# Wider stationary values, a split of the lower parts, and a moved division in an attention and two-network kernel

## The chip, the cores and the metric

The kernel runs on one core of a Trainium2 chip. The metric is the device time of one execution in microseconds (us), the median of several runs.

## The reference

Three stages follow each other. The first is an attention with feature maps: for every head, `proj = x @ w_phi` is shifted by its largest absolute value per token, and the features are `exp` of it and of its negative, side by side. Keys and values are summed up into one matrix per head, and queries read from that.

```
q_p, k_p = phi(q), phi(k)                    # 8 batches, 8 heads, 576 tokens, 2 x 128 features
kv  = einsum('bhsf,bhsd->bhfd', k_p, v)
num = einsum('bhsf,bhfd->bhsd', q_p, kv)
den = einsum('bhsf,bhf->bhs', q_p, k_p.sum(2)) + 1e-6
x   = num / den                              # 4608 tokens of 512
```

The second stage sends each token to one of eight expert networks (or past them), the third is `(h - tanh(h)) @ w_out` with `h = x @ w_in`. All is float32.

## The kernel before, in words

The attention runs as 32 steps over `i`. A step treats two heads of one batch. Two batches share nine tiles of 128 tokens, so a step with even `i` takes five tiles, the last of which counts for 64 tokens only, and a step with odd `i` takes 64 tokens of that same tile, kept in slot 4, and then four full tiles (`slots_of`, L295). The loop is software pipelined: step `i` finishes batch and heads `i`, and prepares `n = i + 1`. The order in which each engine works is the order in which the calls stand in the loop; waits between engines come from the data.

Products are taken in pieces: a float32 is split into a rounded upper part (type FP32R) and the rest, the lower part, and a product is upper x upper, upper x lower and lower x upper. So there are `kh`/`kl`, `qh`/`ql` (`split_qk`, L226), `vh`/`vl` (`split_v`, L239, on GpSimd), and `kph`/`kpl` for the features of the keys: `exp_k` (L269) and `high_kp` (L273) run on ScalarE, `low_kp` (L277) on VectorE, each once for either sign `s`.

TensorE's order in step `i` is: `project(n, "k")` (L245), which fills the PSUM tile `proj`; `transpose_q(i, 0)` (L283); `key_value(i)` (L300); `transpose_q(i, 1)`; the first two tiles of `project(n, "q")`, which overwrite `proj`; `key_value_t(i)` (L315), which multiplies the turned `kv` by a small matrix; the rest of `project(n, "q")`; in one step of eight the two counts of `route_count` (L438); `numerator(i)` (L326) into the PSUM tile `num`. `key_value` forms, per head, three products over the five slots, 15 matmuls in one accumulation: 65 columns of `vh` or `vl` (64 values and a one) are stationary, 256 features move, and 64 or 128 rows (tokens) are summed over.

VectorE's order is: `shift(n, "k")` (L256: maximum over `proj` and subtraction into `dk`), `divide(i - 1)` (L338: reads `num`, writes rows of `x` and of the gate logits), a part of `narrow` (L190, which turns the weights of the last stage from doubles into float32), a part of the routing (L368 to L459), the copy of `kv` from PSUM (L323), `shift(n, "q")`, and `low_kp` for both signs. GpSimd does `kl`, `vh` and `vl`, `ql`, two operations of `narrow` (L212, L213) and the scatters of finished rows. `proj`, `num`, `kvb`, `kph` and `kpl` exist once.

Behind the loop come the expert networks and the last network, which the diff touches in comments only.

Of the kernel before, what the change touches and what calls it, by code (L numbers as in the profile page):

```python
# [8 lines left out]
F32 = mybir.dt.float32  # L9
F32R = mybir.dt.float32r  # L10
# [3 lines left out]
ALU = mybir.AluOpType  # L14
# [5 lines left out]
P = 128  # L20
# [8 lines left out]
NCH = SP // P  # L29
# [8 lines left out]
NSEG = 6144  # L38
BIG = 65536.0

# columns of the constants
C_ID = 0
C_TRI = 128
C_ONE = 256
# [15 lines left out]
def attention_moe_moe_kernel(  # L60
# [52 lines left out]
        eng.dma_start(raw[j // 2][:, o : o + 2048], src(s))  # L113

    def load_w(src, j, when):
        # half of the weights
        with tc.If(when > 0):
            for a in (2 * j, 2 * j + 1):
                load_part(src, a)
# [7 lines left out]
    def expert_w(i):  # L127
        return lambda s: wall[bass.ds(i, 1), :, s].rearrange("o p f -> (o p) f")

# [1 line left out]
    actx = ExitStack()  # L131
    rctx = ctx.enter_context(ExitStack())
    rt = rctx.enter_context(tc.tile_pool(name="route", bufs=1, side="right"))
# [13 lines left out]
    wpl = ap.tile([P, 2 * NF], F32R, name="wpl")  # L147
    wpr = ap.tile([P, 2 * NF], F32, name="wpr")
    wg = ap.tile([P, H, VE], F32, name="wg")
    vh = ap.tile([P, NCH, 2, VD], F32R, name="vh")  # L150
    vl = ap.tile([P, NCH, 2, VD], F32R, name="vl")
    kph = ap.tile([P, NCH * 2, 2, NF], F32R, name="kph")
    kpl = ap.tile([P, NCH * 2, 2, NF], F32R, name="kpl")
    ke = ap.tile([P, NCH * 2, 2, NF], F32, name="ke")
# [13 lines left out]
    st = {}  # L168
    NS = 4 * B

    # Two batches share nine tiles of 128 tokens: an even step takes the first five, an odd step
    # the other four and the fifth's second half, which stays in slot 4.
    def tiles(i):
        return NCH - i % 2

# [12 lines left out]
            )  # L188

    def narrow(w, e, m, x, dve=False):  # L190
        # a double's two words -> the nearest float32, |w| below 2**-106 to 0
        w = w.rearrange("p (n t) -> p n t", t=2)
        low, high = w[:, :, 0].bitcast(U32), w[:, :, 1].bitcast(U32)
        nc.vector.tensor_scalar(  # L194
            out=e, in0=high, scalar1=0x7FF00000, scalar2=None, op0=ALU.bitwise_and
        )
        nc.vector.tensor_scalar(  # L197
            out=m, in0=high, scalar1=0xFFFFF, scalar2=None, op0=ALU.bitwise_and
        )
        yield  # L200
        nc.scalar.activation(e, e, AF.Relu, scale=8.0, bias=bias[:, 0:1])
        nc.scalar.activation(x, low, AF.Identity, scale=2.0**-32, bias=bias[:, 1:2])  # L202
        if not dve:
            nc.scalar.copy(m.bitcast(F32), m)
        yield
        nc.vector.scalar_tensor_tensor(  # L206
            out=e, in0=high, scalar=0x80000000, in1=e, op0=ALU.bitwise_and, op1=ALU.bitwise_or
        )
        if dve:
            nc.vector.tensor_tensor(out=x, in0=x, in1=m, op=ALU.add)  # L210
        else:
            nc.gpsimd.tensor_tensor(out=x, in0=x, in1=m.bitcast(F32), op=ALU.add)  # L212
        nc.gpsimd.tensor_tensor(out=x, in0=x, in1=e.bitcast(F32), op=ALU.mult)  # L213
        yield
# [23 lines left out]

    def split_v(i):  # L239
        n = tiles(i)  # L240
        src = st[i]["v"][:, :n].rearrange("p c (h w) -> p c h w", h=2)
        nc.gpsimd.tensor_copy(vh[:, :n], src)
        nc.gpsimd.tensor_tensor(out=vl[:, :n], in0=src, in1=vh[:, :n].bitcast(F32), op=ALU.subtract)

    def project(i, w, lo_c=0, hi_c=NCH):  # L245
        hi, lo = st[i][w + "s"]
# [22 lines left out]
    def exp_k(i, s):  # L269
        n = tiles(i) * 2  # L270
        nc.scalar.activation(ke[:, :n, s], st[i]["dk"][:, :n], AF.Exp, scale=1.0 - 2.0 * s)

    def high_kp(i, s):  # L273
        n = tiles(i) * 2
        nc.scalar.copy(kph[:, :n, s], ke[:, :n, s])

    def low_kp(i, s):  # L277
        n = tiles(i) * 2
        nc.vector.tensor_tensor(  # L279
            out=kpl[:, :n, s], in0=ke[:, :n, s], in1=kph[:, :n, s].bitcast(F32), op=ALU.subtract  # L280
        )

# [10 lines left out]
            nc.scalar.activation(qp[h][:, s, :n], t[:, :n], AF.Exp, scale=1.0 - 2.0 * s)  # L293

    def slots_of(i):  # L295
        # slots in the order of the tokens, and the partitions that belong to the batch
        full = [(c, slice(0, P)) for c in range(4)]
        return [(4, slice(64, P))] + full if i % 2 else full + [(4, slice(0, 64))]

    def key_value(i):  # L300
        for h in range(2):
            n = 0
            for a, b in ((vh, kph), (vl, kph), (vh, kpl)):
                for c, q in slots_of(i):
                    nc.tensor.matmul(
                        kvb[:VD, h * 256 : h * 256 + 256], a[q, c, h],
                        b[q, 2 * c + h].rearrange("p s f -> p (s f)"),
                        start=n == 0, stop=n == 3 * NCH - 1,
                    )
                    n += 1  # L310
# [2 lines left out]
        nc.scalar.copy(kvt[i % 2][:VD], kvb[:VD])  # L313

    def key_value_t(i):  # L315
        # [feature, value | 1 | value . gate and skip weights]
        for a in range(4):
            nc.tensor.matmul(
                kvb[:, a * VE : a * VE + VE], kvt[i % 2][:, a * NF : a * NF + NF],
                wg[:, i % 8 // 2 * 2 + a // 2], start=True, stop=True,  # L320
            )
        kv = sm.tile([P, 4 * VE], F32, name="kv")
        nc.vector.tensor_copy(kv, kvb[:, : 4 * VE])  # L323
        st[i]["kv"] = kv
# [162 lines left out]
        return cnt, key  # L487

    def first_expert():
        # head: expert, rows of it already placed (256 at most), first row, second tile's row  # L490
        v = nc.vector
        cnt, key = counts_key()
        mx = rt.tile([P, 1], F32, name="kmx")
        v.tensor_reduce(out=mx, in_=key, axis=AX.X, op=ALU.max)
        v.tensor_tensor(out=forced, in0=key, in1=mx.to_broadcast([P, E]), op=ALU.is_equal)
        t = rt.tile([P, E], F32, name="kt")
        v.tensor_tensor(out=t, in0=forced, in1=cst[:, C_EID : C_EID + E], op=ALU.mult)
        v.tensor_reduce(out=head[:, 0:1], in_=t, axis=AX.X, op=ALU.add)
        v.tensor_reduce(out=head[:, 1:2], in_=cnt, axis=AX.X, op=ALU.max)
        v.tensor_scalar(  # L500
            out=head[:, 1:2], in0=head[:, 1:2], scalar1=float(NEARLY), scalar2=None, op0=ALU.min
        )
        v.tensor_scalar(
            out=head[:, 2:3], in0=head[:, 0:1], scalar1=float(CAP), scalar2=None, op0=ALU.mult
        )
        v.tensor_scalar(
            out=head[:, 3:4], in0=head[:, 1:2], scalar1=-float(P), scalar2=0.0, op0=ALU.add, op1=ALU.max
        )
        v.tensor_copy(headi, head)

    def block_table():
        # for each tile of 128 rows: its first row in xs, in x2s, whether an expert starts, the
        # next expert, whether there is one, whether there is none, all tiles
        v = nc.vector
        cnt, key = counts_key()
        done = rt.tile([P, E], F32, name="done")
# [96 lines left out]
        nc.vector.tensor_copy(mt, kvb[:7, :MAXT])  # L613

    def gather_index(seg0):
        # slot -> row of x2s: the first expert's early rows lie in front
        v = nc.vector
        low = rt.tile([P, 3], F32, name="low")
        t = rt.tile([P, E], F32, name="lowt")
# [42 lines left out]
    nc.vector.memset(num[64:, :, (NCH - 1) * VE : NCH * VE], 1.0)  # L662
    for t in kvt:
        nc.gpsimd.memset(t[64:], 0.0)
    split_qk(0, "k", nc.vector)
    split(wpr, wph, wpl)
    project(0, "k")
# [25 lines left out]
    for i in range(NS):  # L693
        n = i + 1
        more = n < NS
        if more:
            project(n, "k")
        if more:
            shift(n, "k")
        if i:  # L700
            divide(i - 1)
        if i == NS - 2:
            ldctx.close()
            bx = rctx.enter_context(tc.tile_pool(name="rows", bufs=1, side="right"))
# [38 lines left out]
        key_value(i)  # L743
        keep_key_value(i)
        if more:
            exp_k(n, 0)
        transpose_q(i, 1)
        if more:
            split_v(n)
            load(n + 1, "v")  # L750
            project(n, "q", 0, QC)
            exp_k(n, 1)
        key_value_t(i)
        if more:
            project(n, "q", QC)
        exp_q(i, 1)
        if more:
            high_kp(n, 0)
            shift(n, "q")
            low_kp(n, 0)  # L760
            high_kp(n, 1)
            low_kp(n, 1)
        else:
            t = pp.tile([P, NCH, 2 * NF], F32, name="proj")
            for c, a in ((0, xr), (1, xt)):
                for k in range(4):
                    nc.tensor.transpose(
                        t[:, 2 * c + k // 2, k % 2 * P : k % 2 * P + P], a[:, k * P : k * P + P], ident
                    )
            split(  # L770
                t[:, :4].rearrange("p (c a) (b f) -> p c (a b f)", c=2, b=2),
                xTh.rearrange("p c k f -> p c (k f)"), xTl.rearrange("p c k f -> p c (k f)"),
            )
# [27 lines left out]
    divide(NS - 1)  # L801
    actx.close()

# [1 line left out]
    wp2 = ctx.enter_context(tc.tile_pool(name="weights2", bufs=1))  # L805
    wh.append(wp2.tile([P, 4096], F32R, name="wh1"))
    wl.append(wp2.tile([P, 4096], F32R, name="wl1"))
    with ExitStack() as bctx:
# [51 lines left out]
            nc.sync.dma_start(x2s[bass.ds(r, P), :], yo)  # L860

        def split_up(half, k, eng):
            # columns of the next expert's first matrix that no later product reads
            cols = slice(half * 512, half * 512 + 512)
            w = [a.rearrange("p (k f) -> p k f", k=4)[:, k : k + 2, cols] for a in (raw[0], wh[0], wl[0])]
            split(*w, eng)
# [81 lines left out]
            nc.vector.tensor_copy(xt, xu)  # L948
    rctx.close()

# [1 line left out]
    op = ctx.enter_context(tc.tile_pool(name="ffw", bufs=1))  # L952
    o2 = ctx.enter_context(tc.tile_pool(name="ff2", bufs=2))
    ph = ctx.enter_context(tc.tile_pool(name="fph", bufs=2, space=PSUM))
# [112 lines left out]
def _layout(np, inputs):  # L1067
    f = np.float32
    q, k, v = (np.asarray(inputs[n]) for n in ("q", "k", "v"))

    # step pairs (two batches, two heads): 1152 tokens
    def feature_major(a):
        t = a.reshape(NPAIR, 2, H // 2, 2, S, DH).transpose(0, 2, 3, 5, 1, 4)
        return t.reshape(NPAIR * H // 2, P, 2 * S)
# [69 lines left out]
```

## Time and profile before

| | |
|---|---|
| three runs | 1605.92, 1611.25, 1613.95 us (median 1611.25) |
| profiled execution | span 1604.1 us (the page has no other time of it) |
| busy: TensorE, weight loads | 1549.3 us (97%), 1286.0 us (80%) |
| busy: VectorE, ScalarE, GpSimd | 839.5 (52%), 630.0 (39%), 393.8 us (25%) |
| granted TensorE clock, mean | 0.987 |

In the profile PE stands for matmuls on TensorE, PEld for loads of the stationary operand, which overlap them; DVE is VectorE, ACT ScalarE, POOL GpSimd. An entry such as `128*65 128x256` is a matmul with 128 rows and 65 stationary columns and an operand of 128 x 256 that moves. A time in front of a timeline row is the start in us from the beginning of the span, the next number is the duration in us. Ends of matmuls are modelled, so their durations overlap; the distance of two starts is the better measure. "L305" is line 305 of the kernel.

### The profile page before, as it was taken

How to read it: one execution, taken by the hardware profiler on the slowest of the kernel's cores; microseconds unless marked ns; L12 is line 12 of the kernel's file. 1: busy time of each engine (PE TensorE's matmuls, PEld its weight loads, DVE VectorE, ACT ScalarE, POOL GpSimd, SP SyncE). 2: the span in 40 equal slices, each digit the busy share in tenths (PEclk: the TensorE clock that was granted, in tenths of full speed). 3: DMA queues.
4: the chain of work that ended last, by engine and by line, in shares of the span. 5: the costliest groups of instructions: out<-in, count | busy, mean ns of one | idle time of the engine just before them, and what ended most of it. 6: DMA issues, size and time to landing. Idle time of an engine off the chain costs nothing.

```text
span 1604.1 us, 23498 instructions
## 1 busy us (share of the span) xinstructions
PE 1549.3 (97%) x8421; PEld 1286.0 (80%) x8421; DVE 839.5 (52%) x1179; ACT 630.0 (39%) x944; POOL 393.8 (25%) x288
## 2 busy tenths in 40 slices
PE   7999999999999999999599999999999999999999
PEld 6888888888887787877488888888888888888887
DVE  5788988988986525435587423232322323232322
ACT  5656556566564123415365322222222222222222
POOL 4444474474466202203423200000000000000000
PEclk9999999999999999999799999999999999999999
DMA  4344365244246513233433201010100101000000
GB/s 148 120 151 158 131 229 200 66 153 159 65 143 231 204 46 137 68 115 137 161 110 117 79 1 53 0 53 0 53 1 7 46 0 54 0 27 1 27 1 27
DMA packets 53576, 139.56 MB, mean 87 GB/s; under 512 B 5488, under 2 KB 5616, under 8 KB 50416
## 3 DMA queue, kind: packets, MB, share of 16 engines
q1 hardware_dynamic: 47152, 116.31, 21.3%
q0 software_dynamic: 5760, 18.90, 3.7%
q10 hardware_dynamic: 576, 3.15, 0.5%
q8 instruction: 59, 0.97, 0.2%
q14 instruction: 29, 0.24, 0.0%
HBM read 86.15 MB, written 52.19 MB: 86 GB/s over the span
## 4 chain that ended last, share of the span: by engine, by line
PE 45%; DVE 2%; POOL 1%; issue 1%; ACT 1%; DMA 0%; POOLq 0%
PE h L1013 22%; PE acc L1029 22%; POOL raw L213 1%; PE xtr L1002 1%; DVE wol L97 1%; DVE raw L210 1%; ACT woh L96 0%; DMA raw<-x2s,gidx 0%; DVE raw L206 0%; POOL raw L971 0%; DVE raw L194 0%; DVE wl L97 0%; ACT raw L202 0%; DVE raw L197 0%; DVE g L1017 0%
## 5 line engine op out<-in xcount | busy, mean ns | idle before, releaser
L1017 DVE TENSOR_TENSOR g<-h,g 128x512 f32<-128x512 f32 x144 | 99.5, 691 | 389.3 <-ACT g L1016 389.3
L1016 ACT ACTIVATE g<-h 128x512 f32<-128x512 f32 x144 | 85.8, 596 | 391.1 <-PE h L1013 391.1
L1013 PE MATMUL h<-x2Th,wh 128*128 128x512 f32 (+1 forms) x580 | 225.8, 389 | 0.0
L1013 PE MATMUL h<-x2Tl,wh 128*128 128x512 f32 (+1 forms) x580 | 225.6, 389 | 0.0
L1013 PE MATMUL h<-x2Th,wl 128*128 128x512 f32 (+1 forms) x580 | 225.6, 389 | 0.0
L1029 PE MATMUL acc<-woh,gh 128*128 128x512 f32 x576 | 225.5, 392 | 0.0
L1029 PE MATMUL acc<-woh,gl 128*128 128x512 f32 x576 | 224.2, 389 | 0.0
L1029 PE MATMUL acc<-wol,gh 128*128 128x512 f32 x576 | 224.1, 389 | 0.0
L333 PE MATMUL num<-kv,qp 128*128 128x74 f32 (+1 forms) x1280 | 151.9, 271 | 3.1 <-DVE kv L323 3.0
L97 DVE TENSOR_TENSOR gl<-g,gh 128x512 fp32r<-128x512 f32 x144 | 101.1, 702 | 98.9 <-ACT gh L96 98.9
L333 PEld LDWEIGHTS num<-kv,qp 128*128 128x128 f32 (+1 forms) x1280 | 139.7, 180 | 14.6 <-DVE kv L323 4.9
L971 POOL DMA_INDIRECT raw<-x2s,gidx x36 | 35.4, 982 | 428.1 <-PE xtr L1002 416.0
L96 ACT CAST gh<-g 128x512 fp32r<-128x512 f32 x144 | 89.4, 621 | 111.0 <-DVE g L1017 111.0
L1013 PEld LDWEIGHTS h<-x2Th,wh 128*128 128x128 f32 x580 | 109.9, 189 | 22.3
L1013 PEld LDWEIGHTS h<-x2Tl,wh 128*128 128x128 f32 x580 | 109.8, 189 | 22.3
L1013 PEld LDWEIGHTS h<-x2Th,wl 128*128 128x128 f32 x580 | 109.7, 189 | 22.3
L1029 PEld LDWEIGHTS acc<-woh,gl 128*128 128x128 f32 x576 | 108.1, 188 | 22.5
L1029 PEld LDWEIGHTS acc<-wol,gh 128*128 128x128 f32 x576 | 108.2, 188 | 22.0
L1029 PEld LDWEIGHTS acc<-woh,gh 128*128 128x128 f32 x576 | 108.1, 188 | 21.9
L279 DVE TENSOR_TENSOR kpl<-ke,kph 128x1280 fp32r<-128x1280 f32 (+1 forms) x64 | 119.9, 1916 | 0.0
L97 POOL TENSOR_TENSOR wl<-raw,wh 128x1024 fp32r<-128x1024 f32 x25 | 66.5, 2682 | 211.8 <-PE y L845 200.8
L293 ACT ACTIVATE qp<-tq 128x640 f32<-128x640 f32 (+1 forms) x128 | 75.6, 643 | 90.6 <-PE tq L287 90.6
(203 smaller groups left out, 2775.6 us busy)
## 6 DMA issues: line engine op xcount, KB each, us to landing
raw<-in_wall_dram SPq DMA_DIRECT2D x20, 1024.0 KB, 5.8
raw<-in_w_dram SPq DMA_DIRECT2D x30, 512.0 KB, 3.7
x2s<-raw SPq DMA_DIRECT2D x12, 1024.0 KB, 5.9
x2s<-x SPq DMA_DIRECT2D x4, 2304.0 KB, 9.6
out_dram<-raw SPq DMA_DIRECT2D x36, 256.0 KB, 3.8
v<-in_vx_dram SPq DMA_DIRECT2D x16, 325.0 KB, 3.0
k<-in_kT_dram SPq DMA_DIRECT2D x16, 320.0 KB, 4.3
q<-in_qT_dram SPq DMA_DIRECT2D x16, 320.0 KB, 3.8
```

The costliest lines, as they stand in the source:

```text
L96: nc.scalar.copy(hi, src)
L97: eng.tensor_tensor(out=lo, in0=src, in1=hi.bitcast(F32), op=ALU.subtract)
L210: nc.vector.tensor_tensor(out=x, in0=x, in1=m, op=ALU.add)
L213: nc.gpsimd.tensor_tensor(out=x, in0=x, in1=e.bitcast(F32), op=ALU.mult)
L279: nc.vector.tensor_tensor(out=kpl[:, :n, s], in0=ke[:, :n, s], in1=kph[:, :n, s].bitcast(F32), op=ALU.subtract)
L293: nc.scalar.activation(qp[h][:, s, :n], t[:, :n], AF.Exp, scale=1.0 - 2.0 * s)
L333: nc.tensor.matmul(o, qp[h][:, s, slot, q], kv[:, a * VE : a * VE + VE], start=s == 0, stop=s == 1,)
L971: nc.gpsimd.indirect_dma_start(out=xg[:, t, :], out_offset=None, in_=x2s[:, :], in_offset=bass.IndirectOffsetOnAxis(ap=gidx[:, b * TB + t ...
L1013: nc.tensor.matmul(p[:, s], a[:, o : o + P], b[:, k, s], start=n == 0, stop=n == 11)
L1016: nc.scalar.activation(g, p, AF.Tanh)
L1017: nc.vector.tensor_tensor(out=g, in0=p, in1=g, op=ALU.subtract)
L1029: nc.tensor.matmul(acc[t], a[:, s], b[:, m], start=m == 0 and n == 0, stop=m == NM - 1 and n == 2)
```

## The change

`vh` and `vl` become flat, with 63 columns of zeros behind them (P - VD), and `key_value` loads 128 columns from the place where the 65 of its slot and head begin. The product then fills all 128 rows of `kvb`; only the first 65 are read, as before. `low_kp` takes an engine; the one for `s = 1` goes to GpSimd, and the order of the calls for the features of the keys changes with it. `divide(i - 1)` stands ahead of `shift(n, "k")`.

```diff
-    vh = ap.tile([P, NCH, 2, VD], F32R, name="vh")
-    vl = ap.tile([P, NCH, 2, VD], F32R, name="vl")
+    vh = ap.tile([P, NCH * 2 * VD + P - VD], F32R, name="vh")
+    vl = ap.tile([P, NCH * 2 * VD + P - VD], F32R, name="vl")
...
     def split_v(i):
         n = tiles(i)
-        src = st[i]["v"][:, :n].rearrange("p c (h w) -> p c h w", h=2)
-        nc.gpsimd.tensor_copy(vh[:, :n], src)
-        nc.gpsimd.tensor_tensor(out=vl[:, :n], in0=src, in1=vh[:, :n].bitcast(F32), op=ALU.subtract)
+        src = st[i]["v"][:, :n].rearrange("p c w -> p (c w)")
+        hi, lo = vh[:, : n * 2 * VD], vl[:, : n * 2 * VD]
+        nc.gpsimd.tensor_copy(hi, src)
+        nc.gpsimd.tensor_tensor(out=lo, in0=src, in1=hi.bitcast(F32), op=ALU.subtract)
...
-    def low_kp(i, s):
+    def low_kp(i, s, eng=nc.vector):
         n = tiles(i) * 2
-        nc.vector.tensor_tensor(
+        eng.tensor_tensor(
...
                 for c, q in slots_of(i):
+                    o = (2 * c + h) * VD
                     nc.tensor.matmul(
-                        kvb[:VD, h * 256 : h * 256 + 256], a[q, c, h],
+                        kvb[:, h * 256 : h * 256 + 256], a[q, o : o + P],
...
+    for t in (vh, vl):
+        nc.gpsimd.memset(t.bitcast(F32)[:, NCH * 2 * VD :], 0.0)
...
             project(n, "k")
+        if i:
+            divide(i - 1)
         if more:
             shift(n, "k")
-        if i:
-            divide(i - 1)
...
         keep_key_value(i)
         if more:
-            exp_k(n, 0)
+            exp_k(n, 1)
         transpose_q(i, 1)
         if more:
             split_v(n)
             load(n + 1, "v")
             project(n, "q", 0, QC)
-            exp_k(n, 1)
+            high_kp(n, 1)
+            low_kp(n, 1, nc.gpsimd)
         key_value_t(i)
         if more:
             project(n, "q", QC)
         exp_q(i, 1)
         if more:
+            exp_k(n, 0)
+            shift(n, "q")
             high_kp(n, 0)
-            shift(n, "q")
             low_kp(n, 0)
-            high_kp(n, 1)
-            low_kp(n, 1)
```

## Rows read from the trace of the kernel before

**Rows 1.** The page: the span and the number of instructions.
```profile
span 1604.1 us, 23498 instructions
```

**Rows 2.** Busy time by stretch: stretch, length, engines (instructions), clock, DMA share, GB/s.
```profile
276.00:340.00 64.00, 62.93 (x478) 53.44 (x477) 59.82 (x80) 38.38 (x54) 33.37 (x25) 1.00 0.31 102
```

**Rows 3.** Waits from 0 to 530 us: who for whom, total, times, longest.
```profile
PEld kvb L305 <- issue: 36.3, 193, 0.3
...
PE num L333 <- DVE kv L323: 3.0, 5, 1.7
...
PE kvb L441 <- DVE kv L323: 1.9, 3, 0.7
```

**Rows 4.** Timeline of TensorE's matmuls from the start of an even step.
```profile
327.46 0.36 PE L252 MATMUL proj<-wph,kh 128*128 128x256 f32 x1
...
327.90 0.28 PE L252 MATMUL proj<-wph,kh 128*128 128x256 f32 x1
...
328.61 0.28 PE L252 MATMUL proj<-wph,kh 128*128 128x256 f32 x1
...
330.35 0.94 PE L305 MATMUL kvb<-kph,vl 128*65 128x256 f32 x5
...
332.09 0.95 PE L305 MATMUL kvb<-kph,vh 128*65 128x256 f32 x5
```

**Rows 5.** Timeline, single instructions: one matmul of 64 rows, then loads.
```profile
330.09 0.33 PE L305 MATMUL kvb<-kph,vh 64*65 64x256 f32 x1
...
330.35 0.13 PEld L305 LDWEIGHTS kvb<-kph,vl 128*65 128x65 f32 x1
330.40 0.14 PEld L305 LDWEIGHTS kvb<-kph,vl 128*65 128x65 f32 x1
330.52 0.14 PEld L305 LDWEIGHTS kvb<-kph,vl 128*65 128x65 f32 x1
...
312.14 0.19 PEld L252 LDWEIGHTS proj<-wph,kh 128*128 128x128 f32 x1
312.25 0.19 PEld L253 LDWEIGHTS proj<-wpl,kh 128*128 128x128 f32 x1
```

**Rows 6.** Groups by shape, 0 to 700 us: count, busy us, mean ns, idle before.
```profile
L253 PEld LDWEIGHTS proj<-wpl,kh 128*128 128x128 f32 x144 | 28.7, 199 | 0.6 <-DVE wpl L97 0.6
...
L305 PEld LDWEIGHTS kvb<-kph,vh 128*65 128x65 f32 x256 | 28.5, 137 | 6.2
...
L234 POOL TENSOR_TENSOR kl<-k,kh 128x640 fp32r<-128x640 f32 x15 | 23.3, 1551 | 23.1 <-ACT kh L233 23.0
```

**Rows 7.** Timeline of VectorE and GpSimd, two places.
```profile
304.33 1.55 POOL L234 TENSOR_TENSOR kl<-k,kh 128x640 fp32r<-128x640 f32 x1
...
304.43 1.48 DVE L420 TENSOR_SCALAR nocs<-nocomp 128x9 f32<-128x9 f32 x1
...
18.81 2.96 DVE L279 TENSOR_TENSOR kpl<-ke,kph 128x1280 fp32r<-128x1280 f32 x2
```

**Rows 8.** Timeline of GpSimd, VectorE and TensorE around one quiet step's end.
```profile
383.46 1.60 POOL L243 TENSOR_TENSOR vl<-v,vh 128x650 fp32r<-128x650 f32 x1
387.42 1.90 POOL L234 TENSOR_TENSOR ql<-q,qh 128x512 fp32r<-128x512 f32 x1 [2.37 <-ACT qh L233]
...
386.68 3.98 DVE L279 TENSOR_TENSOR kpl<-ke,kph 128x1280 fp32r<-128x1280 f32 x2
390.59 1.21 DVE L260 TENSOR_REDUCE mk<-proj 128x8 f32<-128x1024 f32 x1
...
392.97 0.16 DVE L346 TENSOR_SCALAR r<-num 128x10 f32<-128x10 f32 x1
...
394.48 0.17 DVE L361 TENSOR_TENSOR L<-num,r 64x18 f32<-64x18 f32 x1
...
391.94 0.94 PE L305 MATMUL kvb<-kpl,vh 128*65 128x256 f32 x5
...
395.96 0.36 PE L252 MATMUL proj<-wph,qh 128*128 128x256 f32 x1
```

## The prediction

> **What bounds the kernel now.** I read the page first, then busy time by stretch, the table of waits, and the timeline of single steps on TensorE. The change touches only the attention stage, the first 510 us of a span of 1604.1 us [rows 1]. In that stage TensorE is the bound: a 64 us stretch of four steps, with routing in it, shows it busy for 62.93 us, VectorE for 59.82 and GpSimd for 33.37 us, at the full granted clock of 1.00, 2.4 GHz [rows 2]. What TensorE loses by waiting for others in the steady part is 3.0 us in five places for the copy `kv` and 1.9 us in three places (in `route_count`) for the same copy, 4.9 us together [rows 3]. So a shorter stage needs a shorter TensorE sequence; relief of VectorE can give at most those 4.9 us.
>
> A step lasts from 312.14 to 327.46, 15.3 us [rows 4, 5]. In each the key-value product runs in groups of five matmuls (four slots of 128 rows, one of 64), six groups per step, and a group takes 0.87 us (two from 330.35 to 332.09) [rows 4]. The projections, also 256 columns wide in the same type but with 128 stationary columns, take 0.71/6 = 0.118 us each (327.90 to 328.61) [rows 4]. Five of those would be 0.59 us, so a group carries 0.28 us of something else. It would be easy to put this down to the 65 columns. The single instructions say otherwise.
>
> Within a group the 128-row loads follow each other at 0.12 us (330.40 to 330.52), the pace of the projections, although they have 65 columns [rows 5]. The loss sits at the slot of 64 rows. The 64-row matmul starts at 330.09, and the next 128-row one not before 330.35, 0.26 us later [rows 4, 5]. The load engine was idle 36.3 us for no named releaser, 193 times, and 192 is 6 groups times 32 steps: once per group it doesn't run ahead [rows 3]. The change keeps slots of 64 rows in all six groups.
>
> **What the change does to the product.** In the run of 128-row slots a load is hidden behind the matmul before it, for 65 columns and for 128 alike, so nothing is gained or lost there. Around a 64-row slot the loads are not hidden, and there their length counts. Right behind such a change of shape the next load of 65 columns is issued 0.05 us after the first (330.35 to 330.40); where the projections begin behind the 64-column products of `num`, a like change of shape, the load of 128 columns is followed by the next one after 0.11 us (312.14 to 312.25) [rows 5]. That is an exposed load of about 0.055 us for 65 columns and 0.11 us for 128, in the same type. The mean record agrees: 137 ns against 199 ns, 62 ns more [rows 6]. So each exposed load becomes longer by 0.055 us.
>
> Exposed are the load of each 64-row slot and that of the 128-row slot behind it. An even step has 6 and 5 of them (its last 64-row slot is followed by a transpose, which isn't changed), an odd step 6 and 6. Over 16 steps of each kind this is 16 x 11 + 16 x 12 = 368 loads, and 368 x 0.055 = 20.2 us more on TensorE, all of it on the path since TensorE is the bound. From above, 62 ns by the records gives 22.8 us. From below, the exposed load may vanish altogether: -20.2 us; and if the change of shape itself became free, 192 groups x 0.28 = -54 us. I take +20.2, because the projection's load is the same operation in the same type behind a like change of shape.
>
> The Trainium skill, "TensorE: Matmul & The Clock Gate", section "Weight-path perf modes — Fast Weight Load (FWL) and DoubleRow", says that a fast load, up to four times as fast, comes into force with 128 weights and a type other than FP32; it also says that the gain comes from several narrow elements in one 32-bit read, which a 32-bit type doesn't have. By the condition alone the 128-column load would take a quarter of 0.11 us, and each of the 368 loads would be shorter than today by 0.03 us: about -10 us, an estimate from that page, and a rival below. The trace doesn't bear it out for this type: the projection's loads meet the condition and take 0.11 us [rows 5], 199 ns in the record [rows 6].
>
> **Half of the lower parts to GpSimd, and the order of ScalarE.** VectorE loses one of two `low_kp` per step. The two take 3.98 us on an odd step beside a busy GpSimd [rows 8] and 2.96 us at the start beside one that only writes [rows 7], so 1.5 to 2.0 us go. GpSimd gains an operation on 1280 (odd step) or 1024 (even step) elements: twice 1551 ns, the row for 640 elements, is 3.1 us, and 2.5 us for 1024 [rows 6]. Four steps add 11.2 us to 33.4 of 64 [rows 2], 44.6 of some 66 then, so GpSimd isn't the bound. Its new operation stands behind `split_v`, and behind it on that queue wait the lower part of `q`, the arithmetic of `narrow` and the scatters, then the next `k`. In a quiet odd step `vl` runs from 383.46 for 1.6 us, so the new one runs from 385.1 to 388.2 [rows 8]. The product that reads it begins at 390.17, and the third group, the first to need it, at 391.94 [rows 8]. ScalarE runs the same operations of the same sizes, one exponential and one cast swapped round; `exp_q` still has two of them ahead of it. Nothing on TensorE waits for this: 0 us, as long as these 3.7 us of margin hold.
>
> What is left to VectorE there can be held up by GpSimd. `low_kp` of the other half is due at 386.68 [rows 8]; GpSimd works until 388.2, and if VectorE must wait for it, it is done by 388.2 + 1.5 = 389.7, still ahead of 390.6, where the pair ended. That VectorE does wait so is seen where a product over 9 elements took 1.48 us (304.43 to 305.91), just as long as GpSimd's subtraction of `k` ran (304.33 to 305.88) [rows 7].
>
> **Division ahead of the maximum.** `divide` takes 1.7 us (from 392.97 until 394.65) and now stands ahead of `shift`, 2.4 us here (390.59 to 393.0) [rows 8]. In the quiet step it can begin at 389.7, and the shift's end moves from 393.0 to 389.7 + 1.7 + 2.4 = 393.8. TensorE needs it at 395.96, when it begins to overwrite `proj` [rows 8], and with the longer product 0.6 us later: 2 us of margin, cost 0. `num` is also free earlier than it was, with `numerator` far off: gain 0. Of the 4.9 us lost at the copies of `kv` I count 4 as recovered, between 0 and 4.9: on steps with routing VectorE arrives late by up to 1.7 us, and it now has 1.5 to 2.0 us less to do and a step longer by 0.6 us. The two small memsets on GpSimd fall into the wait for the first loads: 0. SP's queue has the same transfers in the same order; those of `v` wait for `split_v`, which keeps its place.
>
> **Sum.** 1604.1 + 20.2 - 4 = 1620 us of span, +16 us. Per step the loads are 11 or 12 x 0.055 = 0.6 us: the odd one from 312.14 to 327.46 becomes 15.9 us [rows 4, 5]. The page has no time of the profiled execution beside its span; the median of the three runs, 1611.25, stands 7.15 us above it, so I put the same difference on top: 1627 us.
>
> **Rivals.**
> - A, the load of 128 columns turns out faster than that of 65, so that the exposed loads shrink. For it: the projections begin behind a different change of shape, so it isn't the very same place. Against it: the 0.11 us above. Between nothing lost and all 20.2 us gone, the middle is -10: 1604.1 - 10 - 4 = 1590, in runs 1597. The fast-load rule above would do just this.
> - B, the full width also frees the change of shape: each group 0.59 us, -54 us. Nothing in the trace speaks for it; the projections pay for their change of shape too, with 128 columns [rows 5]. Then VectorE's chain decides: the shift would be needed at 395.96 - 1.7 = 394.3 and ends at 393.8, so that any hold-up by GpSimd counts; with 1 us given back in half of the steps, 1604.1 - 54 - 4 + 16 = 1562, in runs 1569.
> - C, the longer loads are hidden after all, as in the runs of 128-row slots: 1604.1 - 4 = 1600, in runs 1607, no change that can be told.
> - D, GpSimd becomes late. Its subtraction beside a busy VectorE may stretch as VectorE's own did (3.98 against 2.96, a third): 4.1 us instead of 3.1, until 389.2; and if it takes the lower part of `q`, 1.9 us [rows 8], ahead of the waiting VectorE, the shift ends at 389.2 + 1.9 + 2.0 + 1.7 + 2.4 = 397.2, past the 396.6 at which TensorE needs it. From there it decides: 0.6 us, with a scatter in between more, say 1 us on each of 16 odd steps on top of the forecast, 1643 in runs. The Trainium skill, "SBUF — State Buffer", section "Who interferes with whom", has this as a rule: an operation of VectorE with two inputs in SBUF and one of GpSimd that reads SBUF exclude each other for a whole instruction. The 1.48 us over 9 elements agree with it.
>
> **Chances.** A difference under 0.5% (8 us) can't be told from none here. Forecast 0.59, D 0.07: slower, 0.66. C 0.18: the same. A 0.09, B 0.07: faster, 0.16. The range goes from inside A, 1592, to just under D, 1641; the forecast's own, from 55 to 62 ns per load and 0 to 4.9 us recovered, is 1627 to 1634, with the 4 us by which the runs scatter 1623 to 1638.
>
> **What would show it.** Right: the groups of five at 0.97 to 0.98 us instead of 0.87, loads of the product in records near 195 ns, the first gap between loads behind a 64-row slot 0.11 us, odd steps of 15.9 us, hardly any wait for `kv`. Wrong: groups at or under 0.87 us (A, B or C), or waits on TensorE for `dk` in `proj` or for `kpl` from GpSimd in the product (D). The time behind the attention stage should not change.

## The result and the profile after

| | median, us | runs, lowest to highest | ratio to before (95%) |
|---|---|---|---|
| before | 1609.55 | 4, 1605.92 to 1613.95 | |
| after | 1623.74 | 4, 1620.18 to 1624.27 | 1.0078 [1.0053, 1.0104] |

The change makes the kernel 0.8% slower by the ratio, 14 us by the medians. The forecast was 1627, and slower by over 0.5% had 0.66 of the chance. The profiled execution of after took 1623.92 us, 2.1 us more than its span.

The page of after, span and busy time by engine. TensorE's matmuls grow by 17.8 us (1549.3 before), about as much as the span (1604.1 before, [rows 1]); VectorE loses 61.7 us and GpSimd gains 65.2; of this the time shows only the waits for `kv` that are gone (below).

```profile
span 1621.8 us, 23528 instructions
...
PE 1567.1 (97%) x8421; PEld 1314.5 (81%) x8421; DVE 777.8 (48%) x1148; ACT 638.3 (39%) x944; POOL 459.0 (28%) x321
```

The same stretch as in [rows 2], after. VectorE has gone from 59.82 to 50.29 us and GpSimd from 33.37 to 39.08 of 64, at the same clock of 1.00. TensorE has no gap left: it was busy for 62.93 and is busy for 64.00.

```profile
276.00:340.00 64.00, 64.00 (x465) 55.81 (x464) 50.29 (x76) 38.16 (x53) 39.08 (x28) 1.00 0.25 81
```

Waits of TensorE from 0 to 540 us, after: all rows that name VectorE. Of the 4.9 us for `kv` in [rows 3], 0.2 is left. There is none for `kpl`, and the one for `dk`, 3.2 us, is the kernel's first step and stood there before.

```profile
PE proj L253 <- DVE dq L265: 3.2, 1, 3.2
PE proj L253 <- DVE dk L265: 3.2, 1, 3.2
PE kvb L444 <- DVE cum L413: 2.4, 1, 2.4
PE proj L254 <- DVE wpl L97: 0.3, 1, 0.3
...
PE kvb L444 <- DVE kv L326: 0.2, 1, 0.2
```

TensorE's timeline after, the start of two steps and groups of one key-value product. The groups of five begin 0.98 us apart (511.50 to 512.48); in [rows 4] it was 0.87. The odd step from 289.03 to 304.99 is 15.96 us long; one was 15.32 [rows 4, 5].

```profile
289.03 0.39 PE L253 MATMUL proj<-wph,kh 128*128 128x256 f32 x1
...
304.99 0.36 PE L253 MATMUL proj<-wph,kh 128*128 128x256 f32 x1
...
510.52 1.04 PE L308 MATMUL kvb<-kph,vh 64*128 64x256 f32 x5
511.50 1.05 PE L308 MATMUL kvb<-kph,vl 64*128 64x256 f32 x5
512.48 1.05 PE L308 MATMUL kvb<-kpl,vh 64*128 64x256 f32 x5
```

The weight loads of the same place, one by one. (Of the second group one record is missing, between 511.91 and 512.15.) Behind the 64-row load 0.31 us pass (0.26 between the matmuls of [rows 4, 5]), and the first gap after that is 0.10 to 0.11 where [rows 5] have 0.05.

```profile
510.52 0.18 PEld L308 LDWEIGHTS kvb<-kph,vh 64*128 64x128 f32 x1 [0.17 <-issue]
510.83 0.19 PEld L308 LDWEIGHTS kvb<-kph,vh 128*128 128x128 f32 x1
510.94 0.19 PEld L308 LDWEIGHTS kvb<-kph,vh 128*128 128x128 f32 x1
...
511.50 0.18 PEld L308 LDWEIGHTS kvb<-kph,vl 64*128 64x128 f32 x1
511.81 0.19 PEld L308 LDWEIGHTS kvb<-kph,vl 128*128 128x128 f32 x1
511.91 0.19 PEld L308 LDWEIGHTS kvb<-kph,vl 128*128 128x128 f32 x1
512.15 0.19 PEld L308 LDWEIGHTS kvb<-kph,vl 128*128 128x128 f32 x1
```

Groups by shape, 0 to 700 us, after: the load of the product (137 ns in [rows 6]) and the lower parts of the features. The two that VectorE did took 3.98 us on a quiet odd step [rows 8]; its one now takes 1.51, and GpSimd's takes 2.91 us for 1280 elements and 2.37 for 1024.

```profile
L308 PEld LDWEIGHTS kvb<-kph,vh 128*128 128x128 f32 x256 | 34.7, 191 | 6.2
...
L280 POOL TENSOR_TENSOR kpl<-ke,kph 128x1280 fp32r<-128x1280 f32 x15 | 43.7, 2911 | 6.4 <-PE proj L255 6.1
L280 POOL TENSOR_TENSOR kpl<-ke,kph 128x1024 fp32r<-128x1024 f32 x16 | 37.9, 2368 | 11.8 <-ACT kph L276 11.8
L280 DVE TENSOR_TENSOR kpl<-ke,kph 128x1280 fp32r<-128x1280 f32 x17 | 25.5, 1506 | 5.8 <-ACT kph L276 5.8
```

Where the time went, from the starts of TensorE's matmuls in the two traces. The key-value product over 32 steps is the time from its first matmul to the next piece of another kind.

| us | before | after | difference |
|---|---|---|---|
| attention, first key-value product to the experts | 487.6 | 500.8 | +13.2 |
| of it, key-value products | 167.8 | 187.0 | +19.2 |
| of it, projections of `q` with the waits for `kv` behind them | 62.77 | 56.83 | -5.9 |
| experts | 289.1 | 292.3 | +3.2 |
| last network | 800.6 | 801.7 | +1.1 |

The turns of `q`, `key_value_t`, `numerator` and the projections of `k` agree to 0.1 us. The runs don't show that the experts' 3.2 us are the change's doing: the same stage took 289.9 us in the kernel with the widening alone and 293.7 in the kernel before with another order of the product, and neither has the rest of the change. The profile of before is of an execution near its fastest (the runs of before take 1.8 us more than their spans; with these the span makes 1605.9, the lowest of its four), so the traces differ by 17.7 us where the medians differ by 14.2.

### The profile page after: what moved, and what is told of

It reads as the page before. It is cut to its first block, busy times and chain, and to the rows that moved or that the text cites. A ratio compares the mean times of both kernels' runs of the same rounds, so it can differ in the third digit from the quotient of the medians.

```text
span 1621.8 us, 23528 instructions
## 1 busy us (share of the span) xinstructions
PE 1567.1 (97%) x8421; PEld 1314.5 (81%) x8421; DVE 777.8 (48%) x1148; ACT 638.3 (39%) x944; POOL 459.0 (28%) x321
## 5 line engine op out<-in xcount | busy, mean ns | idle before, releaser
L336 PEld LDWEIGHTS num<-kv,qp 128*128 128x128 f32 (+1 forms) x1280 | 139.7, 180 | 10.7 <-DVE kv L326 0.2
L280 POOL TENSOR_TENSOR kpl<-ke,kph 128x1024 fp32r<-128x1024 f32 (+1 forms) x31 | 81.6, 2631 | 18.2 <-ACT kph L276 11.8
```

What stands on the lines that cost most here:

```text
L280: eng.tensor_tensor(out=kpl[:, :n, s], in0=ke[:, :n, s], in1=kph[:, :n, s].bitcast(F32), op=ALU.subtract)
L336: nc.tensor.matmul(o, qp[h][:, s, slot, q], kv[:, a * VE : a * VE + VE], start=s == 0, stop=s == 1,)
```

## The experiments

Each ratio is to the runs of before that were taken beside it. Their medians were 1610.23 us (20 runs; the kernel without the widening, the widening alone, wide only where exposed, 96 columns), 1609.19 us (19 runs; step 28's lower part on VectorE, the two with the 64-row matmuls last in each head, both heads together) and 1610.76 us (9 runs; the last three). "Key-value" is the 32 products' time as in the table.

**The change without the widening.** After, with 65 columns.

```diff
-                        kvb[:, h * 256 : h * 256 + 256], a[q, o : o + P],
+                        kvb[:VD, h * 256 : h * 256 + 256], a[q, o : o + VD],
```

> The changed kernel with 65 stationary columns again; GpSimd's half of the lower parts and the early division stay. Theory (the longer loads at the 64-row slots carry the whole loss, the rest of the change gives back the waits for kv): groups of five at 0.87 us, odd steps 15.3 us, about 20 us below the changed kernel, 1604 us, some 5 us (0.3%) faster than before. Rival (GpSimd's half or the early division costs time): no faster than before, 1609 us or more, with waits of TensorE for kpl or proj.

Measured: 1611.42 us (1608.98 to 1612.91), ratio 1.0005 [0.9996, 1.0014]. Key-value is back at 166.8, so the widening alone lengthens the products. But the expected gain is missing. The steps run at 15.33 and 14.88 us, those with `route_count` up to 0.8 us longer, with one exception: the step with `i` = 28 and the next take 20.25 and 17.20, which is 7.2 us more than their kind. In step 28 VectorE does the arithmetic that picks the first expert. The rows below (timeline of all engines; then three stretches of 5 us, columns as in [rows 2]) show a conversion of 4 elements taking 2.34 us, as long as GpSimd's new subtraction that began 0.04 us before it. The copy of `kv` comes 2.25 us later than the conversion began, TensorE waits for 2.52 us, and then the granted clock is near 0.5, 1.2 GHz, for 10 us: `numerator` starts at 457.94, and the next step's first matmul comes 7.39 us later; in after the 40 matmuls of `numerator` take 4.75 us.

```profile
455.14 2.35 POOL L280 TENSOR_TENSOR kpl<-ke,kph 128x1024 fp32r<-128x1024 f32 x1 [0.86 <-ACT kph L276]
455.18 2.34 DVE L512 CAST headi<-head 128x4 int32<-128x4 f32 x1
...
457.43 0.45 DVE L326 COPY kv<-kvb 128x296 f32<-128x296 f32 x1
...
457.94 7.46 PE L336 MATMUL num<-kv,qp 128*128 128x74 f32 x40 [2.52 <-DVE kv L326]
...
465.33 0.58 PE L253 MATMUL proj<-wph,kh 128*128 128x256 f32 x1
```

```profile
455.00:460.00 5.00, 2.48 (x20) 2.27 (x18) 4.93 (x6) 4.97 (x8) 3.36 (x2) 0.93 0.00 0
460.00:465.00 5.00, 5.00 (x25) 4.58 (x25) 1.61 (x2) 0.69 (x2) 4.23 (x4) 0.50 0.85 228
465.00:470.00 5.00, 5.00 (x25) 4.43 (x24) 2.55 (x7) 0.25 (x1) 1.31 (x2) 0.55 0.86 296
```

In after the same two operations miss each other by 0.9 us (timeline of VectorE, GpSimd and TensorE): the conversion ends at 472.82, and GpSimd's begins at 473.70. It is held up there too, but only by what is left of the subtraction before it, which ends at 472.80.

```profile
471.47 1.33 POOL L244 TENSOR_TENSOR vl<-v,vh 128x520 fp32r<-128x520 f32 x1
...
472.28 0.54 DVE L512 CAST headi<-head 128x4 int32<-128x4 f32 x1
...
473.31 0.47 DVE L326 COPY kv<-kvb 128x296 f32<-128x296 f32 x1 [0.48 <-PE kvb L321]
...
473.70 2.36 POOL L280 TENSOR_TENSOR kpl<-ke,kph 128x1024 fp32r<-128x1024 f32 x1 [0.90 <-ACT kph L276]
...
473.83 4.75 PE L336 MATMUL num<-kv,qp 128*128 128x74 f32 x40
```

**The same, with step 28's lower part left on VectorE**, to see whether that one meeting is what is missing.

```diff
-            low_kp(n, 1, nc.gpsimd)
+            low_kp(n, 1, nc.vector if i == NS - 4 else nc.gpsimd)
```

> The changed kernel with 65 columns, and in step 28 alone both lower parts on VectorE. The run with 65 columns alone came out at 1611 us instead of the 1604 expected; its trace has one wait of TensorE for kv of 2.5 us in step 28, where small operations of VectorE stand still beside GpSimd's, and a granted clock of 0.5 for 10 us behind it; that step and the next are 7.3 us too long. Theory (GpSimd's new operation causes the wait, the wait the low clock): both go, 1604 us, 0.4% faster than before. Rival (the low clock and the 6 us have another cause, or the rest of the change costs them): 1610 us again.

Measured: 1607.40 us (1602.80 to 1609.71), ratio 0.999 [0.9977, 1.0003]. Step 28 and the next take 16.55 and 15.32 us, no stretch of low clock is left in the attention, and that stage takes 482.8 us where before has 487.6. The conversion takes 0.17 us here. A wait of 1.5 us for `kv` is left, as VectorE's own lower part (1.22 us) now stands ahead of the copy, without a low clock behind it. So the meeting was the cause of the low clock in the trace. Against the runs of before beside each, 3.0 of the 7.2 us came back (1.2 us above them, then 1.8 below), and the split and the moved division together aren't told from nothing.

**The widening alone.** Before, with `vh`, `vl` and the product as in the change, and nothing else of it.

```diff
-                        kvb[:VD, h * 256 : h * 256 + 256], a[q, c, h],
+                        kvb[:, h * 256 : h * 256 + 256], a[q, o : o + P],
```

> The kernel before with nothing but the 128 stationary columns. Theory: groups of five at 0.98 us, about 20 us more on TensorE; VectorE has 0.6 us more per step, so some of the 5 us of waits for kv go by themselves: 1625 to 1630 us. Rival (the loss comes from the other parts of the change): 1609 us, as before.

Measured: 1622.27 us (1619.33 to 1623.44), ratio 1.0071 [1.0057, 1.0085]. Key-value 187.2, as in after. TensorE still waits for `kv`, for 1.7 us instead of 4.9: the longer product by itself gives VectorE time. So the products grow by 19.4 us, the attention by 15.4 in the trace, and the medians differ by 12.0; the trace of before is of an execution of 1605.92 us, 4.3 under the median of those beside, which is most of the rest.

**Wide only where the loads are exposed**: the 64-row slot and the one behind it. (One matmul more per head is wide in odd steps, the last, which closes the accumulation.)

```diff
-                for c, q in slots_of(i):
+                for j, (c, q) in enumerate(slots_of(i)):
                     o = (2 * c + h) * VD
+                    w = P if n == 3 * NCH - 1 or j in ((0, 1) if i % 2 else (0, 4)) else VD
...
-                        kvb[:, h * 256 : h * 256 + 256], a[q, o : o + P],
+                        kvb[:w, h * 256 : h * 256 + 256], a[q, o : o + w],
```

> The changed kernel with 128 columns only in the loads at a change of shape (the 64-row slots and the 128-row slot behind each, and for the form of the accumulation the last matmul of a head in odd steps), 13 or so of 30 per step; the others have 65. Theory (only those loads are exposed): as the changed kernel, 1623 us, groups of five at 0.98 us. Rival (every one of the 30 wider loads costs its 20 ns): 13/30 of the loss, about 1612 us, groups near 0.92 us.

Measured: 1624.39 us (1620.99 to 1624.88), ratio 1.0081 [1.0067, 1.0095], key-value 186.6. Over half of the matmuls are at 65 columns again, and 0.4 of the 19.2 us comes back: width counts only at the changes of shape. A loss spread evenly over all loads would have given more than half of it back.

**96 columns**, for the law between 65 and 128.

```diff
-                        kvb[:, h * 256 : h * 256 + 256], a[q, o : o + P],
+                        kvb[:96, h * 256 : h * 256 + 256], a[q, o : o + 96],
```

> The changed kernel with 96 stationary columns instead of 128. Theory (an exposed load takes time in proportion to its columns): 31/63 of the 20 us, so 1613 to 1614 us, groups at 0.92 us, first gap between loads behind a 64-row slot about 0.08 us. Rival (what counts is only whether the width is that of the array): 1604 or 1624 us.

Measured: 1614.99 us (1612.06 to 1616.22), ratio 1.0025 [1.0015, 1.0034], key-value 177.2, 9.4 of the 19.2 us at 31 of the 63 columns. The three widths lie on a straight line, and 128 isn't a special number for this type. The records agree: 137, 163 and 191 ns.

**Before, with the 64-row matmuls last in each head**: one stretch of them per head instead of three.

```diff
-            for a, b in ((vh, kph), (vl, kph), (vh, kpl)):
-                for c, q in slots_of(i):
+            for slots in (full, half):
+                for a, b in prods:
+                    for c, q in slots:
...
```

(`full` are the slots of 128 rows, `half` is the one of 64, and `prods` the three pairs of operands.)

> The kernel before with the order of the 15 matmuls of a head changed: the twelve of 128 rows first, the three of 64 rows last, so two changes to 64 rows per step instead of six. Theory (the 0.28 us per group is the change of shape, the 65 columns have no part in it): 4 x 0.28 x 32 = 36 us less on TensorE; VectorE, at 54 to 60 of 64 us, then becomes the bound on steps with routing and gives some back: 1575 to 1585 us. Rival (the 0.28 us belongs to each matmul of 64 rows, wherever it stands): 1610 us.

Measured: 1598.26 us (1591.55 to 1601.46), ratio 0.9932 [0.9908, 0.9957]. Key-value falls by 34.2 us, to 133.6, with the same matmuls: it is the change of shape that costs, not the 64-row matmul wherever it stands. But only 11 us arrive, against 24 to 34 expected. Steps without routing take 14.18 and 13.75 us, and in these VectorE with both lower parts is late where routing comes on top: waits for `kv` of 13.0 us in the first two rows below (TensorE, 0 to 540 us), and granted clocks of 0.95 and 0.81 in the stretches shown.

```profile
PE num L337 <- DVE kv L327: 10.3, 7, 2.8
...
PE kvb L445 <- DVE kv L327: 2.7, 3, 1.2
```

```profile
276.00:340.00 64.00, 61.69 (x478) 56.58 (x477) 56.36 (x79) 38.43 (x55) 38.22 (x31) 0.95 0.33 111
404.00:468.00 64.00, 60.00 (x402) 55.07 (x401) 48.48 (x80) 31.61 (x45) 30.54 (x25) 0.81 0.28 91
```

**After, in the same order**, still 128 columns.

```diff
-            for a, b in ((vh, kph), (vl, kph), (vh, kpl)):
-                for c, q in slots_of(i):
+            for half in range(2):
+                for a, b in prods:
+                    for c, q in slots_of(i):
+                        if (c == 4) != bool(half):
+                            continue
...
```

> The changed kernel, 128 columns kept, with the same order (three matmuls of 64 rows last in each head). Theory: the exposed loads fall from 11.5 to 4 per step and the changes of shape from 6 to 2: 36 us for the shape, 13 us for the loads, less VectorE's work: about 1623 - 49 = 1574 us, if nothing else becomes late. Rival (wide loads cost the same everywhere): 1623 - 36 = 1587 us.

Measured: 1585.60 us (1582.11 to 1591.17), ratio 0.987 [0.984, 0.9901]; key-value 138.1. Two things follow. The width now costs 4.5 us instead of 19.2 (138.1 against 133.6; 5.8 if every step had the median product of its kind), because fewer loads are exposed. And the split, the moved division and ScalarE's order together are worth their place in these shorter steps, as 1585.6 against 1598.3 says in spite of the wider loads. The one long wait is step 28's again, 4.1 us; that step takes 22.14 us and the next 15.75, 9.6 us more than their kind. So the time came out at the rival's 1587 us and not at the theory's 1574, though the products are short as the theory has it.

**Both heads' 64-row matmuls together at the end of the step**, in one accumulation, 65 columns (from after).

```diff
-        for h in range(2):
-            n = 0
...
-            for a, b in ((vh, kph), (vl, kph), (vh, kpl)):
-                for c, q in slots_of(i):
...
+        n = 0
+        for half in range(2):
+            for a, b in prods:
+                for h in range(2):
+                    for c, q in slots_of(i):
+                        if (c == 4) != bool(half):
+                            continue
...
-                        start=n == 0, stop=n == 3 * NCH - 1,
+                            start=n == 0, stop=n == 6 * NCH - 1,
```

> The changed kernel with 65 columns and all six matmuls of 64 rows of a step together at the end, both heads in one accumulation. Theory: one change of shape per step instead of six, 5 x 0.28 x 32 = 45 us off the 1604 to 1611 us of the run with 65 columns: 1560 to 1566 us, if VectorE and GpSimd keep up with steps of 13.5 us; a wait of a few us in steps with routing, with a low clock behind it, would make it 1570 to 1580. Rival (as above): 1605 us.

Measured: 1583.98 us (1578.59 to 1586.16), ratio 0.9855 [0.983, 0.9879]; key-value 123.1, 44.7 less than before, as worked out; the time is above both ranges that were expected. In step 28 a multiplication over 8 elements takes 2.28 us beside GpSimd's 2.36 (timeline), TensorE waits for 5.70 us, and the step lasts 23.22 us instead of 13.46.

```profile
427.45 2.36 POOL L280 TENSOR_TENSOR kpl<-ke,kph 128x1024 fp32r<-128x1024 f32 x1
427.55 2.28 DVE L503 TENSOR_TENSOR kt<-forced,cst 128x8 f32<-128x8 f32 x1
...
431.76 8.68 PE L339 MATMUL num<-kv,qp 128*128 128x74 f32 x40 [5.70 <-DVE kv L329]
```

The stretch behind that wait, columns as in [rows 2]: the clock is 0.52 for 11 us.

```profile
432.00:443.00 11.00, 11.00 (x54) 10.43 (x55) 4.75 (x9) 0.00 (x0) 3.78 (x4) 0.52 0.75 246
```

**The same, with step 28's arithmetic behind the copy of `kv`** (and the three loads of values that read it).

```diff
-        if i == NS - 4:
-            first_expert()
...
         transpose_q(i, 0)
...
             low_kp(n, 0)
...
+        if i == NS - 4:
+            first_expert()
...
```

> The run with both heads' 64-row matmuls together (1584 us), with first_expert in step 28 behind the copy of kv instead of ahead of it. In that run TensorE waits 5.7 us there, while VectorE's product over 8 elements stands 2.3 us beside GpSimd's new subtraction, and the granted clock is 0.5 for 13.7 us behind the wait: steps of 23.2 and 14.9 us instead of 13.5 and 13.9. Theory (the wait brings the low clock, both go when the copy isn't behind those operations): 10 us less, 1574 us. Rival (the low clock comes anyway, or the wait moves to proj): 1580 us or more.

Measured: 1575.76 us (1568.15 to 1580.09), ratio 0.9786 [0.9765, 0.9806]. Step 28 takes 13.62 us and its low clock is gone: 8 us between the medians, 9.8 against the runs of before beside each, for moving a dozen tiny operations. Another such stretch, behind the first `route_count` (step 10, 18.56 us), stays.

**`numerator`'s 64-column products last, too**, so that it changes shape once per step.

```diff
-        for h in range(2):
-            for c, (slot, q) in enumerate(slots_of(i)):
+        for half in range(2):
+            for h in range(2):
+                for c, (slot, q) in enumerate(slots_of(i)):
+                    if (slot == 4) != bool(half):
+                        continue
...
```

> The same, and the eight products of num with 64 columns together at the end of numerator, one change of shape less per step. Theory (a change costs the same whether rows or columns halve; the trace of before has 0.09 us to enter and 0.09 us to leave above the usual distance): 0.18 x 32 = 6 us less than the run before it, 1568 us. Rival (only the change of rows costs): no difference, 1574 us.

Measured: 1574.32 us (1573.96 to 1574.56), ratio 0.9773 [0.976, 0.9787]. Steps without routing become 0.36 and 0.27 us shorter (13.54 and 13.19; 0.18 was expected), some 10 us over 32 steps, but the median moves by 1.4 us only, which the intervals don't tell from none. The three steps with `route_count` now take 18.88, 18.60 and 18.68 us: a wait of 1.3 us for `kv` in each, and a low clock behind each. The kernel ahead has the same three waits in its trace and a low clock of that kind behind one of them. Why it is three here stays open. Below, the wait of the third and the 10 us that follow.

```profile
PE kvb L450 <- DVE kv L329: 3.9, 3, 1.3
```

```profile
397.00:407.00 10.00, 10.00 (x53) 9.71 (x53) 5.69 (x11) 3.54 (x6) 6.61 (x4) 0.53 0.20 61
```

**The routing's arithmetic behind the copy of `kv`, its counts at the start of the next step.**

```diff
-        if phase == 2:
-            routing = route_rank(*routing)
         if phase == 3:
+            routing = route_count(*routing)
             route_slot(*routing)
...
         if phase == 2:
-            routing = route_count(*routing)
+            routing = route_rank(*routing)
```

> The same, and in the steps with routing route_rank behind the copy of kv, and route_count one step later. The run with both heads' slots together waits 2 to 5 us in each of three such steps, once with a low clock of 10 us behind it (steps of 18.5, 15.4 and 15.4 us instead of 13.5). Theory: these go too, 7 to 9 us less than the run before it, 1560 us. Rival (VectorE has no room left, the wait moves into the next step): no difference.

Measured: 1577.58 us (1575.74 to 1580.51), ratio 0.9795 [0.9779, 0.9811]: a miss, the rival was right. (The 2 to 5 us of the expectation are by how much those steps were too long; the waits for `kv` in them were 1.3 us each.) Nothing waits for `kv` in those steps any more, but the counts stand in `kvb`, and the next product overwrites it as soon as VectorE has read them. These waits are longer (TensorE, 0 to 540 us), and steps of 21.3 to 21.7 us take the place of those of 18.7.

```profile
PE kvb L311 <- DVE runb L454: 17.6, 3, 5.9
```

## Why the prediction was right

- **The bound.** Right: the 61.7 us taken from VectorE gave back no more than the waits of TensorE for it, some 5 us in the trace, and adding to TensorE's sequence moved the end.
- **Where the loss sits.** Right, and shown from two sides: width at other slots costs nothing, and the same matmuls with fewer changes of shape save 34.2 and 44.7 us of the products' time.
- **20.2 us for longer loads.** Measured 19.2 against before and 20.2 against the same kernel with 65 columns (187.0 against 166.8), and 19.7 against either without the first step, whose product takes longer than the others of its kind in before and after; per load 0.052 to 0.055 us. The estimate from the projection's load, in the same type behind another change of shape, held. That the time is the load's follows from the records and the gaps; the runs don't tell a load from another part of the change of shape that would grow with the columns. Rivals A, B and C fall with this. The rule named beside rival A, of the Trainium skill, "TensorE: Matmul & The Clock Gate", section "Weight-path perf modes — Fast Weight Load (FWL) and DoubleRow", doesn't show for this type: its condition alone would have made 128 columns cheaper than 96, and the runs give a straight line; its remark that a 32-bit type has nothing to win agrees with them. The rows print these operands as f32, so whether the projection's loads meet the condition at all, as the prediction has it, stays open.
- **4 of 4.9 us of waits recovered.** 4.7 in the trace, and 5.9 by the starts of the matmuls (the row of `q` in the table). But not all of it is the split's: the widening by itself took 3.2 of the 4.9.
- **GpSimd's half at no cost.** Right for this kernel, by less than the prediction thought. The operation takes 2.91 and 2.37 us (3.1 and 2.5 predicted), and nothing on TensorE waits for it. Rival D looked for the trouble in the subtraction of the lower part and the shift of the quiet odd step; where it did come, once the steps were as short as before, was a tiny operation of step 28, even, ahead of the copy of `kv`, with GpSimd's operation begun a moment earlier. The prediction had the lock and a row of it [rows 7], and did not go through the small operations that stand between GpSimd's new place and the copy. Nor did it price what follows a wait: 2.5 us of waiting cost 7. The 1.48 us that it sets beside rival D's rule are of an operation with one input ([rows 7], `nocs<-nocomp`), so they say nothing of that rule's two inputs; the 2.28 us of `kt<-forced,cst` above, which has two, agree with it.
- **Division.** No wait for `dk` behind it: 0, as said. It wasn't tried by itself.
- **The sum.** The step of 7.15 us from the span to the median was wrong by its size. An execution takes 2 us more than its span (1623.92 against 1621.8); the rest was that the profiled one was among the shortest of before. In terms of differences the forecast was +16 us, all of it in the attention. There the traces gave 13.2: the loads came out 1.0 us under the 20.2, and the gain was 5.9 instead of 4. Another 4.3 us stand behind the attention, where the prediction had nothing, so that the 17.7 of the whole trace and the 14.2 of the medians came closer to 16 than the attention alone; that part is luck.

## What to carry to other kernels

Before widening or narrowing an operand, look at the distances between single matmuls: where loads are hidden, width is free both ways, and where they aren't, the remedy is fewer changes of shape, not another width. Here a changed order of the same matmuls gave 0.7% by itself (1598.26 us), and 2.3% (1574.32 us) together with the split, the moved division and step 28's arithmetic behind the copy, where the width took 0.7% by itself. When a step gets shorter, go through every small operation that stands ahead of the copy that the bounding engine needs, and count a wait there at two to three times its length where a low clock follows: 2.5 us cost 7.2 and 5.7 us cost 10.7 here, over the step and the next.

## What the runs showed of the hardware

- A wait of TensorE of 1.3 to 5.7 us in a busy stretch was followed, in many of these cases, by a granted clock near 0.5, 1.2 GHz: 2.52 us and then 10 us of it in the kernel without the widening; 5.70 and then 11 in the one with both heads together. Not each was: in the variant with step 28's lower part on VectorE a wait of 1.5 us wasn't, nor in before one of 1.7 us [rows 3]. After, without such waits, keeps 1.00 through the attention.
- An operation of VectorE over 4 or 8 elements took 2.34 and 2.28 us beside a GpSimd subtraction of 2.35 and 2.36 us that had begun 0.04 and 0.10 us earlier; the first takes 0.17 in the variant where GpSimd does nothing at that time. The Trainium skill, "SBUF — State Buffer", section "Who interferes with whom", says that whoever issues first keeps the shared ports for a whole instruction; the trace agrees, and shows that the one that waits can be as small as 4 elements.
- A stationary FP32R operand of 65, 96 and 128 columns is loaded in records of 137, 163 and 191 ns, and what an exposed load adds grows with its columns in a straight line: 19.2 us for 63 columns more, 9.4 for 31, over 368 loads.
- A change between 128 and 64 rows and back costs some 0.28 us with 256 columns that move. Going from six of them per step to one saved 44.7 / (32 x 5) = 0.28 us each, the figure that [rows 4] gave.
